# Threshold attention followed by a maxout FFN on one core: both r of a quad share one pass over the ninth keys

## The chip, the cores and the metric

The kernel runs on one core of one Trainium2 chip. Times are device microseconds of one execution of the whole program, and the figure of a version is the median of its runs.

## The reference

```python
# attn: q, k, v are (8, 8, 576, 64) f32, tau = 0.02
scores = scale * np.matmul(q, k.transpose(0, 1, 3, 2))          # scale = 1/8
thresh = np.max(scores, axis=-1, keepdims=True) - tau
scores = np.where(scores >= thresh, scores, -1000000000.0)
scores = scores - np.max(scores, axis=-1, keepdims=True)
attn = np.exp(scores)
attn = attn / (np.sum(attn, axis=-1, keepdims=True) + 1e-09)
o = np.matmul(attn, v)
# ffn: x is o as (4608, 512); w1, w2, w3 are (512, 768), w_out is (768, 512)
h = np.maximum(np.maximum(x @ w1, x @ w2), x @ w3)
out = h @ w_out
```

Each of 64 heads (8 batches of 8) takes a 576 by 576 softmax in which only scores within tau of the row's maximum count. The FFN works on the 576 tokens of each batch, 512 wide.

## The kernel before

**Tiling.** A batch is split into two quads of four heads. In a quad, heads are numbered 2r + i, with r = 0, 1 and i = 0, 1. The 576 tokens of a batch lie nine to a partition (64 partitions of nine), so that the first eight make four chunks of 128 and the ninth tokens make a chunk of 64. For a quad there are nine steps of scores: four chunks of 128 queries for i = 0, one step that takes the ninth queries of both i (64 rows each), and four chunks for i = 1. Each step has two halves, r = 0 and 1.

**A half of scores (S).** `scores` multiplies queries with all 576 keys in f32. The keys lie in two row halves of PE (partitions 0 to 63 and 64 to 127), 320 and 256 of them, and the two halves of the array run side by side into two PSUM banks. The trace prints the shape of the array as 64*128. The step of the ninth queries is split by columns as well, 64*64. The result `sc` is 128 by 576.

**Softmax.** `maximum` (m, on DVE) writes z = -sc with the row's minimum beside it. Then one of two ways, set for each half by a digit in `MASKED`. Unmasked: `threshold` (s, DVE, a small instruction), `exponents` as a Prelu with a very small slope (e, ACT) and `numerators` as an Exp with a running sum (n, ACT). Masked: `exponents` as an Exp (e, ACT) and `numerators` as a compare and multiply with a sum (k, DVE). So an unmasked half costs two passes over 128x576 on ACT and one on DVE, a masked one costs one on ACT and two on DVE. Digits 2 and 3 are the same two ways with the e step reading `sc` from PSUM (2 has no threshold step). Then `reciprocals` (r, DVE), and `normalized` (p, POOL) writes `P` in bf16. When both r are there, a DMA on SP turns `P` (t) into `ptq`, a tile of 128 by 9 by 1152: nine chunks of 128 keys, 576 queries for each i. Chunks 0 to 3 hold the keys of r = 0, chunks 5 to 8 those of r = 1, and chunk 4 holds the ninth keys of both, r = 0 in partitions 0 to 63 and r = 1 in 64 to 127.

**The product (O).** `product(L, r, ...)`, line 415, makes the output of one r. It goes over five chunks: m = 0 to 3 with weights `vb` (v of the eight tokens, cast on POOL) and m = 4 with `vrb`, the v of the ninth tokens. i = 0 goes to PSUM partitions 0 to 63 and i = 1 to 64 to 127, so the array is 128*64, and the two i run side by side. Since chunk 4 holds the keys of both r, `vrb` has zeros in the rows of the other r (three buffers `vr0` to `vr2`, lines 244 and 661 to 666, zeroed once by DVE; `cast_v` fills the rows). Each pass runs over 576 query columns as 512 and 64, since a PSUM bank holds 512. The result `o` is copied to `xt` by DVE for r = 0 (w) and by ACT for r = 1 (x).

**FFN.** `hid` makes `ph` for each of six blocks of the hidden width and three weights. Both 64-row halves of the contraction run side by side (64*128), in two steps F and B with the halves exchanged. ACT copies the first (h), DVE takes the maximum (v). `outp` makes `po`, which ACT copies to `ob` (u) for the store (o). The last batch (7) is split in two parts of 256 and 320 tokens (`SPLIT`), whose FFN has the shapes 128*128.

**PSUM.** Four tags `s0` to `s3` of 1024 f32 columns, two banks each; this document calls such a tag a bank pair. Every S, T (transposes of q and k, `tp`), O and F step takes the pair that the digit behind its letter names, and waits until its last user has been read.

**The order.** Nothing schedules at run time. `ORDER` is one string of letters; `issue` (line 719) takes them one after the other, and `_Ordered` (line 84) keeps each engine to that order. `products` (line 692) hands out the O steps, two per quad (r = 0, then r = 1), and in the string other letters can stand between the two. The other letters are a, c (copies of `tp`), q (swaps on POOL), y (casts of v), l, g (loads), z (weight casts), i, d (stores) and N, j (the ninth tokens' outputs). All instructions show line 93 in the profile, since `_Ordered` issues them; they are told apart by their tiles.

Of the kernel before, what the change touches and what calls it, by code (L numbers as in the profile page):

```python
# [12 lines left out]
BF16 = mybir.dt.bfloat16  # L13
# [8 lines left out]
FLAT = 2.0 ** -100  # L22

MASKED = """
232222322322222222021032222202332122123122200200111000000000100000000011
000010111020011000101000000001100001001000010011111100000000100100000000
110010030111000100010000000001010100001110001011010100110000000000000000
100101101011000000120000001010000000110011100000001110001000010011111021
"""


# [6 lines left out]
SPLIT = {7: ((0, 1), (2, 3, 4))}  # L38

ORDER = """  # L40
llllllglllT0laclT1laclzllqqS0qqS1meS2mS3lmlT0enlkS1ylmlT2eamelrnpS3leqlmnyS1qcapS0emtnrcS3pmnT2qmepgrelS1qya
gS0pmelT2mqnS3tcpemqS2nlkT1eytaS0rmnT1kpermS3yS2enczrmS1qT0enmepnqtS3nprmaymgpeS0lptS2mppT0mtpS1enencnqsS3re
rmtpS0mS1penmS3lqnsS2mtperpekzllmT0tmpenkT1pgS3eearnS0petmnqrS2meqlnpS3lmnplsS2cetpremS1pS0nmplermtzeS3mnS2p
mtnpmS3rkpS1leektS0emnrpmemptS1eekS2pO3mktS0rennmpermT2pnS1wptemS3prkyO0tmeakS2pgS1enxlnrmS0lpesS2mezT3mS1np
mgntspcS2eqrseT3mtpeS0srmapS1mnT2ptS3mnqO0ceqmeO1prswnptnkS3pxS0meF1meS2zBresmT0qghF3klpF2nkBtaS1sveS0pemF3B
nyrrsmyBepT1svS0hpcT2nS3zmaS1erpgsF2mntpsBmnS3yvF1etssT0myeBprS2cnpS3mnS0ympelF2epF3lmBnzslssvS0htBrqmeS2vpn
S1gF0sepmF3teqBmF2erssvpBtnBkphF0eS1vtS3znmF2nrBmqteS1rpvBnS3pmlnF0pmgeS1qsBsrhmS3pevS2npS1mF0npsO3ermpesmO2
zewepgsskBxtT3nF1vS2nklBarS0mlphS3mtepF2sS1rmnyBmetF3pvT0eBpcnS2tzT1nvS0asmzS3temS2qeS1meF0trkpmS3lenpBmnlys
reklpF1umerpskS3upBeoketmS0uS2umpS3tesmS1qeT0myO2nqlrsnlprcO3etqsmepwS0xptS1mnF3psnmS2BlerskpS1thF0meF3pmeBF
2ktnBveBsrS1nvpS0hmyF3emF2npBrssT0eprtvBaF1kS3nqvBeF0myhyS2kyleF3mBelBvnpS2snsS0vptemS1pnF3rmpT2tnBmpeF0scS1  # L50
htBrnmpF3erT2rpvlBasS1pstvnS2pmeF0pS3emtBqnmT2S1hcqS3empF2eS0rsqmtS1epsmBeF3pmnF0stsvBeBknF2klhF1BvelS0nrvpB
emT3pS2arvS0ptnS3mpnO1smtesrkpeF2swnlrpmeT0S1qtescS3epBmnpmnT0trskS3paS1umS0ulqmeS3lmyS1nopS2smelS0rmeS3psmn
O1ypersmqO2etkpemO0lewqxlknpS3tS1keF2momS3lexF0ktT1enkBercpnsBpumN1ertkphkF3jS0rursS1empBnmF2ptS0vpS1smeF3yt
BsnsmBpnvS0pT1hmF2atT3srepS0cF1eprBsmeqF3vnByBynvplS2nsS0plmhS1mteS2mF0nF3mteS1rrspBnmS2pelvBlepF1smT0leqBvl
aS2rkhF3oqnsS0mtS1epmBeqsF2ssmtS0epvBeyF1mnF3vpBesrS0ktphBermS1npT2svO0nytmpncT3eS1wF2nrmS0aBrsmnqF3vnT1pS0c
eBptsF2mhpS1eS3pmteS0qmBeO1spmnkteF3rvnpT0BsskapS2xvS0erS1qmtnS3pmnF2mqlespmeS1rtkBepresmT3puS1cuS0ptmnS3pS2
meyS1lrekpF0tnsmempO3lekteskO2nrsmpeBkpxrnwS1uptS3muS2pnmF0yoeS1mF3lesymBtnS2srkpS1hmBeF0spveF2ertBmpT3nrsvS
1paBlmpnS0tS3qhmF1epsmS2leBymF3tevF0nBknlS1rsvpS2esmqnBF3srmhpS1epS0tmeF2pssBrempBtesvS0ynF1mT3lnpBvF0lhsrcS
2tnT1mBnF3valS2nrBsqmeF0pvS1epS2meBptsmS3eqF1hmT2peBcS3tnskT2O0arkplnmO2lerpvewptS3xkpS1nF2meF0sstreBsmpS3nv
pBnmS1tS2hmT3eF0rmpnF1cBpnBrevptT3S2apvS0qmtS3S1enmqF2esrsqmiepmleS0soykeS1plBnmemtS3ukS0uT1snrlO2cpekynO1me  # L60
ymeF3pwxskteS0keS1BrrnkopmF2pmS0BqeuurtsmF1phS3srnpS2meT0ptBmeS3ykpaN2esvempF0tS1jkpF3ermBeS2ptvnS1pmBnS0rls
hsmpS2elF3mqntS1mpF0nsrBskpeF2lsmBetBpveF1yhvS3lnkS2lesF0mytnBmBerqsS3veF2lpvnF1pBsmT0htBceF3rT2vnpBsaS0pvnF
1qmtS2nBsrnmT0pS3hrcpF2esS1mpteS0rmpS3emBpntF1svqnS0ssBmpeoT2vO3lamtneF1wS0nrlBpmeS3qsrS2hsmS0pnmF1eptS3smeB
pmF2ntS0veS3rsmnpS1BnpO0veytrempS2empS3xsmS1tekF0nsknlT2rmpBelmlpnscS3quS1umyS2eorT0kpeO3tmeyO1ewlepsmF3etka
rknS2qklT0nBmxespcS2eryF0mpF1uskpuBtnS2BhmqF3nsvS0peS2srmtpF1eBmpeF0srvnBptS2hyS3pmeF1lmeBlBevtF3nkT2S0arrvp
BnS2mphS1smpF0ntS3smnpBmeF1lsT2esvlF3nrBrcptBnvpS2eS0qmlhS1tsnprsmT3F2epmS0aptBemF3yevS1oS0nqmBnpsrS2mnF1ptv
S0epmBeS3mthS2skeF0F1snmlBeklO3ersvpnrmByepF0swT2eqtBvnqF3ssrcS1hpiBmpT0S2vaptS1snmS0pnT3mqF2tecT1BarmS3pnS1
vqeS0mF2pesrmnptmS3npT1seS0qctBeymqermpS1eS3mpuF0nmtuskS1eS2klnS3smBesrsepO1upmemO2txrkpukeO3wnkpS0xS2emF3et
rmS1pnBssspmF2hS0rtepS3mnBpmF1etS0veF3mnN2rnpBpjF0evtF2esBkBkhF1nsvS3eBmBevO3hrkS2pwnS1mnF3prmS2eptsF0mnBpsS
1sevyS2terBmpeF3svS1iyepBmoS0yhmtF2ekF3nBsmS1ersBvpnF0pmeF2BvteS1hBmF3rsS0vpeF1rknpBBmnO2vhptO0xrpnS3pwS2trm  # L70
npS0mnF3pmteF1pBeBvtS0rS2vpS3empF1ktkF0kBereskpemBkperumO2uptO3xpN1wtenkO2jrF3pxF1hpF2nvF3tvF1rhF2pvF3pvF1hF
2tvF3vF1hF2voF3vF1ohF2vF3vF1hF2vO3vO1wF2xuuF1oF0hiF3vF1vF0hF3vF1vF0hF3vF1vF0hF3vF1vF0hF3vF1vF0huF3vF1ovF3uoF
0uoN1fjdi
"""


# [28 lines left out]
def kernel(  # L105
# [34 lines left out]
    one = ctx.enter_context(tc.tile_pool(name="one", bufs=1))  # L140
# [100 lines left out]
                               in_=v[b].rearrange("h (p c) d -> p c h d", c=9)[:, 8])  # L241
                yield

    vrs = [one.tile([128, 4, D], BF16, name=f"vr{x}") for x in range(3)]

    def cast_v(L):
        L["vb"] = vp.tile([128, 4, 4, D], BF16, name="vb")
        pool.tensor_copy(out=L["vb"], in_=L["vm"])
        yield
        L["vrb"] = vrs[(2 * L["b"] + L["qd"]) % 3]  # L250
        for r in range(2):
            rows = slice(64 * r, 64 * r + 64)
            pool.tensor_copy(out=L["vrb"][rows, 2 * r:2 * r + 2], in_=Ls[2 * L["b"]]["vr"][rows, 4 * L["qd"] + 2 * r:4 * L["qd"] + 2 * r + 2])
            yield

    def half(n, i):
# [155 lines left out]
            L["pt"] = pt_pool.tile([128, 9, W], BF16, name="ptq")  # L412
        sync.dma_start_transpose(out=L["pt"][:, :, c["idx"] * 128:(c["idx"] + 1) * 128], in_=c["P"])

    def product(L, r, target, part=None):

        pt, vb, vrb = L["pt"], L["vb"], L["vrb"]
        st = {}

        lo, hi = span(part)  # L420
        n = min(hi, 512) - lo
        base = 448 if ninth_first(L["b"]) else 0
        if ninth_first(L["b"]):
# [218 lines left out]
    Ls, xts, stores, stores9, ends, ninths = {}, {}, [], [], [], []  # L642
# [147 lines left out]
    x = 0  # L790
# [39 lines left out]
```

## Time and profile before

| | |
|---|---|
| runs | 446.49, 447.15, 447.59 us; median 447.15 |
| the profiled execution | 446.69 us, of which its span is 444.8 |
| granted TensorE clock, mean | 0.988 |
| busy: PE, PEld, DVE, ACT, POOL | 422.4, 320.2, 392.8, 403.0, 311.9 us |
| products: `o` from `vb`, `o` from `vr` | 544 and 136 matmuls |

Busy time is the union of the instructions of an engine, and the ends of matmuls are modelled: a matmul's row is longer than its share of the array, and successive rows overlap. Starts are the better guide to what a matmul costs. PEld is the weight load, which overlaps PE. A form such as 128*64 is the tile shape of the array, rows by columns; 128x512 is partitions by elements of the moving operand.

### The profile page before, as it was taken

Reading aid. Unit: us, or ns where it says so; the run is one execution under the profiler, and the core shown is the slowest. Engines: PE = TensorE matmul, PEld = TensorE weight load, DVE = VectorE, ACT = ScalarE, POOL = GpSimd, SP = SyncE. Lnnn points to the kernel's source line nnn. Section 1 sums busy time; section 2 is a strip of 40 time slices with the busy share of each in tenths; the row PEclk is TensorE's granted clock in tenths of the full one; section 3 lists DMA queues with packets and bytes.
Section 4 is the critical chain, followed back from the end, with each engine's and each line's share of the span. In section 5 each row is a group of like instructions: output and inputs, shape, how many; then the busy total and the mean of one; then the engine's idle time right before and its main releaser. Section 6 shows DMA issues by size and latency. Waiting matters only on the chain.

```text
span 444.8 us, 14254 instructions
## 1 busy us (share of the span) xinstructions
PE 422.4 (95%) x5188; PEld 320.2 (72%) x5190; DVE 392.8 (88%) x1228; ACT 403.0 (91%) x836; POOL 311.9 (70%) x420
## 2 busy tenths in 40 slices
PE   7767789999999999999999999999999999999996
PEld 6334347787788767787788777788688886787873
DVE  3887999999999999999999999998999998899642
ACT  3999999999999999999999999899999999987632
POOL 2799989997878687696785877676676685457400
PEclk8998999999999999999999999999999999999999
DMA  7999999999999999699899999989999977487633
GB/s 188 275 293 199 291 169 269 235 243 262 229 180 194 212 222 292 125 256 167 143 234 189 230 198 203 209 168 210 208 206 194 244 151 105 83 179 136 145 116 108
DMA packets 213959, 88.50 MB, mean 199 GB/s; under 512 B 189184, under 2 KB 202240, under 8 KB 213888
## 3 DMA queue, kind: packets, MB, share of 16 engines
q1 hardware_dynamic: 213360, 86.96, 95.9%
q8 instruction: 41, 0.67, 0.6%
q10 hardware_dynamic: 528, 0.62, 0.5%
q14 instruction: 30, 0.25, 0.2%
HBM read 35.65 MB, written 9.44 MB: 101 GB/s over the span
## 4 chain that ended last, share of the span: by engine, by line
PE 86%; ACT 5%; DVE 4%; issue 2%; DMA 1%; SPq 0%; DVEq 0%; ACTq 0%
PE ph L93 32%; PE sc L93 32%; PE po L93 10%; PE o L93 9%; ACT z L93 5%; PE tp L93 3%; DVE z L93 3%; DMA qm<-in_q_dram 1%; ACT qt L93 1%; SPq L93 0%; DVE xt L93 0%; DVE hm L93 0%; DVE stage L93 0%; DVE rs L93 0%; ACT ob L93 0%
## 5 line engine op out<-in xcount | busy, mean ns | idle before, releaser
L93 POOL TENSOR_SCALAR P<-z,rs 128x576 bf16<-128x576 f32 x250 | 200.6, 814 | 63.3 <-DVE rs L93 28.1
L93 DVE TENSOR_SCALAR_CACHE_REDUCE z<-sc 128x576 f32<-128x576 f32 x250 | 183.7, 750 | 14.8 <-PE sc L93 10.1
L93 PE MATMUL sc<-kt,qs 64*128 64x256 f32 (+2 forms) x640 | 182.6, 423 | 5.7 <-DVE z L93 2.3
L93 PE MATMUL sc<-kt,qt 64*128 64x320 f32 (+2 forms) x640 | 182.4, 433 | 5.2 <-ACT z L93 3.3
L93 PE MATMUL ph<-xt,w 64*128 64x288 bf16 (+2 forms) x2160 | 170.8, 283 | 0.1
L93 PEld LDWEIGHTS <-w 64*128 64x128 bf16 (+1 forms) x2160 | 130.1, 94 | 28.6 <-issue 4.3
L93 ACT ACTIVATE z<-z 128x576 f32<-128x576 f32 x174 | 117.6, 679 | 0.1
L93 PEld LDWEIGHTS sc<-kt,qs 64*128 64x128 f32 (+1 forms) x640 | 92.4, 180 | 25.7 <-DVE z L93 5.7
L93 ACT ACTIVATE z<-z,th 128x576 f32<-128x576 f32 x143 | 106.2, 769 | 5.0 <-DVE th L93 4.2
L93 PEld LDWEIGHTS sc<-kt,qt 64*128 64x128 f32 (+1 forms) x640 | 91.9, 179 | 19.7 <-ACT z L93 5.9
L93 DVE SCALAR_TENSOR_TENSOR z<-z 128x576 f32<-128x576 f32 x76 | 62.2, 830 | 0.5 <-ACT z L93 0.5
L93 PE MATMUL po<-wo,hT 64*128 64x512 bf16 (+3 forms) x454 | 53.5, 354 | 0.3
L93 POOL COPY qs<-qt 64x640 f32<-64x640 f32 (+3 forms) x66 | 43.0, 652 | 10.8 <-ACT qt L93 7.2
L93 ACT ACTIVATE z<-z,nm 128x576 f32<-128x576 f32 x68 | 50.6, 767 | 0.0
L93 DVE TENSOR_TENSOR hm<-ph,hm 128x576 bf16<-128x576 f32 (+2 forms) x54 | 37.0, 686 | 9.2 <-PE ph L93 8.9
L93 ACT ACTIVATE hm<-ph 128x576 bf16<-128x576 f32 (+2 forms) x54 | 31.8, 589 | 13.4 <-PE ph L93 12.8
L93 POOL TENSOR_SCALAR P<-stage,rs 128x576 bf16<-128x576 f32 x38 | 30.4, 804 | 19.3 <-ACT z L93 5.4
L93 PEld LDWEIGHTS <-hT 64*128 64x128 bf16 (+2 forms) x456 | 30.0, 95 | 16.5 <-issue 2.3
L93 DVE TENSOR_TENSOR hT<-ph,hm 128x576 bf16<-128x576 f32 (+2 forms) x54 | 37.0, 686 | 4.0 <-PE ph L93 2.3
L93 PE MATMUL o<-ptq,vb 128*64 128x64 bf16 (+2 forms) x544 | 39.0, 281 | 0.0
L93 ACT ACTIVATION_READ_ACCUMULATOR z<-z 128x1 f32 x174 | 34.3, 197 | 0.0
L93 PEld LDWEIGHTS <-vb 128*64 128x64 bf16 x544 | 23.3, 111 | 12.8 <-issue 4.9
(45 smaller groups left out, 431.6 us busy)
## 6 DMA issues: line engine op xcount, KB each, us to landing
vm<-in_v_dram SPq DMA_DIRECT2D x32, 256.0 KB, 4.8
qm<-in_q_dram SPq DMA_DIRECT2D x15, 512.0 KB, 5.0
km<-in_k_dram SPq DMA_DIRECT2D x15, 512.0 KB, 5.3
out_dram<-ob SPq DMA_DIRECT2D x14, 512.0 KB, 4.0
stage<-in_moe_w_dram SPq DMA_DIRECT2D x9, 512.0 KB, 5.2
ptq<-P SPq DMA_TRANSPOSE x144, 4.0
vr<-in_v_dram SPq DMA_DIRECT2D x16, 128.0 KB, 3.4
stage<-in_moe_w_out_dram SPq DMA_DIRECT2D x3, 512.0 KB, 4.9
```

Source lines behind the costliest of these rows:

```text
L93: ins = fn(*a, **kw)
```

## The change

`product` makes four passes for each r. The ninth keys of both r are done in one pass after the four of r = 1: r = 0 in rows 0 to 63 of the array and r = 1 in rows 64 to 127, each i in its own 64 columns, thus four matmuls in 64*64 quadrants for each run of columns. Rows 0 to 63 write the bank pair that r = 0's step took, rows 64 to 127 that of r = 1, so r = 0's result is complete only after r = 1's step. `vrb` needs only two heads' width and no zeros: each half of its partitions holds the two heads of its r. `start` is set for the first matmul in each bank alone. `MASKED` has other digits and `ORDER` is another string with the same letters but for four (86 k and 202 n become 90 and 198, and 169 s become 168).

```diff
@@ MASKED, ORDER: new strings (not shown) @@
-    vrs = [one.tile([128, 4, D], BF16, name=f"vr{x}") for x in range(3)]
+    vrs = [one.tile([128, 2, D], BF16, name=f"vr{x}") for x in range(3)]
...
-            pool.tensor_copy(out=L["vrb"][rows, 2 * r:2 * r + 2], in_=Ls[2 * L["b"]]["vr"][rows, 4 * L["qd"] + 2 * r:4 * L["qd"] + 2 * r + 2])
+            pool.tensor_copy(out=L["vrb"][rows], in_=Ls[2 * L["b"]]["vr"][rows, 4 * L["qd"] + 2 * r:4 * L["qd"] + 2 * r + 2])
...
-    def product(L, r, target, part=None):
+    def product(L, r, target, part=None, other=None):
...
-        order = [(m, run) for m in range(5) for run in runs] if part is None else \
-            [(m, run) for run in runs for m in range(5)]
+        order = [(m, run) for m in range(4) for run in runs] if part is None else \
+            [(m, run) for run in runs for m in range(4)]
...
             for m, (*q0, p0, n) in order:
+                opens = m == 0 and (p0 == runs[0][2] or p0 // 512 != runs[0][2] // 512)
                 for i in range(2):
-                    w = vb[:, 2 * r + i, (1, 3, 0, 2)[m], :] if m < 4 else vrb[:, 2 * r + i, :]
-                    tensor.matmul(ps[64 * i:64 * i + 64, p0:p0 + n], w,
-                                  pt[:, 4 if m == 4 else m + 5 * r, q0[i]:q0[i] + n],
-                                  start=(m == 0), stop=(m == 4))
+                    tensor.matmul(ps[64 * i:64 * i + 64, p0:p0 + n], vb[:, 2 * r + i, (1, 3, 0, 2)[m], :],
+                                  pt[:, m + 5 * r, q0[i]:q0[i] + n], start=opens, stop=False)
+            if other is None:
+                return
+            for *q0, p0, n in runs:
+                shuts = p0 == runs[-1][2] or p0 // 512 != runs[-1][2] // 512
+                for x, two in ((0, other.st["ps"]), (1, ps)):
+                    rows = slice(64 * x, 64 * x + 64)
+                    for i in range(2):
+                        tensor.matmul(two[64 * i:64 * i + 64, p0:p0 + n], vrb[rows, i, :],
+                                      pt[rows, 4, q0[i]:q0[i] + n], start=False, stop=shuts)
...
+        p.st = st
...
-    plain = vrs[2].rearrange("p h d -> p (h d)")[:, 0:128]
+    plain = vrs[2].rearrange("p i d -> p (i d)")
     vector.memset(vrs[2], 0.0)
-    for t in vrs[0:2]:
-        for x in range(2):
-            vector.memset(t[64 - 64 * x:128 - 64 * x, 2 * x:2 * x + 2, :], 0.0)
...
                 for g in (2 * b, 2 * b + 1):
-                    for r in range(2):
-                        yield product(Ls[g], r, x_of, part)
+                    p = product(Ls[g], 0, x_of, part)
+                    yield p
+                    yield product(Ls[g], 1, x_of, part, p)
```

More of the change, by code (lines that the diff above doesn't have):

```diff
@@ L24 @@
 MASKED = """
[L25 to L28, printed above, removed]
+032222120132222220001212222202110312323122222200113000000010000000100001
+000010011010011000011000000010100001011000110001011110000000100010000010
+110000001110000101010000000101001000001001011001031020011000100000000010
+001100111100001000000002001010000000011110101001100010110000001101011122
 """
@@ L40 @@
 ORDER = """
[L41 to L70, printed above, removed]
@@ L71 @@
-npS0mnF3pmteF1pBeBvtS0rS2vpS3empF1ktkF0kBereskpemBkperumO2uptO3xpN1wtenkO2jrF3pxF1hpF2nvF3tvF1rhF2pvF3pvF1hF
-2tvF3vF1hF2voF3vF1ohF2vF3vF1hF2vO3vO1wF2xuuF1oF0hiF3vF1vF0hF3vF1vF0hF3vF1vF0hF3vF1vF0hF3vF1vF0huF3vF1ovF3uoF
-0uoN1fjdi
+lllllllgllT0laclT1qqS0lacllzlqqS1msS2emS0lmelT3nlkT1lyrmlS2eaacqlcqS3mlqS1yenmnpS0mpemS1ytS2enrqmpT3nmS1pler
+sS2pleklpaS0gmnT3teqrmeqclpemS3ngkpS1temT2myT0teacS2qrenkynS0mqeS3rmpnS1ymprenT3ptmS2npsS1ersmzetT0mS2epT1al
+pmnS3lyscnleS0qrmtepS3epmgnS2pktzeamS1leknS0qnrmepnS3ptmprmS2preemtpT1mS3ptenncS0npsrS1mepmtS3eqmS0ezS2nkT1p
@@ new lines @@
+nrmnpstmeqemS0prklptS3emeankpS1gemlerS2kptrmS0penmeS3ptmnpreS1mpelS2mqtS0kpO3emS1rktpmO2enkqgenemnlS0rlnwplx
+rprS3mteS2pmnT0pS1mntT3psmS2apersS1cepS3meO0zmekpO1gmtkzS3T2enxswntS1ceF0psrF2meqlBmnqgF3rhsBktyeT1svByaF0pv
+nT2pS1rncS3pterBmpS2hsmF1petT0sS3mpaBepsmF0eT2zvBncF3pgnS1vlS2ynrmBtnS0pmhS1sysmeS2zremF0pgS3esmtBpesmF2pnS1
+vBqesmF0nyF3klnBsstrS1vepBmhpF2nrlvS0pnS1lmpBelrmS3zetS0vF1nqmF2nptBmeS3qssBhkqgF0evS1eBrpssmeS2pmnO3pveS1rn
+mpF0nmS2zeBmS1pgnssrkO2tyhesmeS0wtpF1esS3pmxBtyremS2pnF0vpT3estmT1zBacS2ezsvtS3emT1qnS0tF2nrmpnmpS3nlS0qmnlB
@@ new lines @@
+rseklpatkF3epemS1urqmS0ueBpokntyS1mupS2usrmlS0peT3lsmeO1qtcnpO2mestkS3xwS0erlsmF1pnS2sspmeBF3rtkhpF0emBnkF1p
+lBnvBerrtS2vphS3mpS0nmF1pteS2mpeBmT0nlF3rsskpeF2tBvaBespvF1onS0ktF3hrmBpeF2rvqeT0BsnycBnsvS0peS1rmqthS3mpeS0
+smF2eypT1mBaptS3snvS1ynmT0qF2nlmpF3elBrscpS1elvyS0nlmBteF2pmF1hsskBnBtsveS3rF0revpF2ekqBnS1mBhmpF3espvS0tnS1
+pmeT2BmytayS0rvnpS1S2semqT3nmO0percptS1mpF3emtenskT2eS1kBarknpmS2urpsS1sumepS3tmepS2mnS1mlS3erslssO2pmelmqek
+S1ptxS3nsmS2ermtO1pewpeO3mylnkleS0ylF2xwtqermpeT3S1cnpBmnqtrkepS3S1umoN0eyskpuemS3F2nrstsmpF1jBkpeF0klhBekF3
@@ new lines @@
+BnsvBrtS2vphS1mepF3mnlS0BsnlrmpF1elsT2vpBatsrF3pvnT2S0prnclByemS1leS2tmpS0hmpF1reslsS2mnpBtmnpS0evS3yqF2smln
+T1qBtmeF0vaT3eBciF2ekS3lhS1rstsmpnBmqS0eS3vpeF1srnmtF2pBnmpBevS3qthsF0mnT1BrkpeF3vaT2BscpeF1rtnS0svpBempS3hr
+S2lymnS0plmS1etqF3mnS2pmeF0trBsempBnsvpT2oO1evteO3knsrkapS0nwF2xmpeskytS1nS0rrmeS3pssemS1pBemptnmT0puS3cuS1y
+tmeqS0S2mnqS3semlyF1nrmpeskO0pesmO2eqktnnS3wBxrkpermS0upS2srsumS3eptmF1epS0mS2epmtBnpsF3mhS0srleBpmT1lnpF2vt
+eS0kS3amBntF1veF0ssBmnBlrekF3pohF2kleBvBespS1vhS0trmepS2rnmpS1nS3smptF0essmqF2nBmpleS1svlS3nBlrmpnF0lrsF1npm
@@ new lines @@
+tBepvT3BhsycF2elrS0vyteS3pmeT1pBmaoF0qevT1tS3npcBsnkF1lS2hrmtpBemT0qnS3vF2qnmO1pesketO3kaesrrpBwxS0ynsvpS1eS
+3mptF2nmqS0nrmBpS1mhqS3temF2pT0snmS1perBscptF3evT0peBsmyS2ntvS1nmF3elskelrS2meplBmnpkatS1uS0umT2eO3slcesrkO1
+permepkS2nF0qtxsemS1pewBympenrkS3ptuS1muS2nmpS0eN3sqmtermpeF2kF0ynBkjS1hT3pmBaS2sstrvepS3reF1mpS0nompF2lnmBp
+F3etvqS0nsBmnS1trsBhkpF0esvF2eBmyeBrkF1phS3vnS2mpntS0mepF3mBelT2srsevF0ptBnrcpF1ekBpoBvhlS2ntpvF3nT0mBaS1rrt
+svpeF2mT0qnS3sclpBesS1lmphS0tmeqF2mnS3pBsnrlssmpF0etS1vqeBmS2evT3F1amS0nsS3qmeS2prBsmnF0ptmhS3qerBssmS2pevS1
@@ new lines @@
+eptS3mnF0ympS2nBtmnO1rvepsnO3kpemeS0rwtpS2xmpnS1smF0lerktepT2knS3meBlcpnmeS1tS2usrmpF3espmeT1sutkO2erkpaO0kl
+nleS1wyxBpsemtnkT0F1urcpS2ulrS0epmoS3nqBstmeF2ysmT0hBqaF3veyS1psS0nmpBerF2kptnF1vBemBphS3srnrtvpS2eF0mpS1nml
+pF3nBssmpeBsrvF1peT2hBycplF0nvS3leBsmelF1vlS2nBtemS0nrsS2pmhS3tqmeF1smpnS2lBqemS3tervS0pF2nsmpT1tnBmyF3avS0e
+tS1keF2rmnpBsBmqhF0rnspssS3veBptmF2epvT1S3nqctBemS0hT1srkF3poaS2meBmqnF0sS1vpnS2rmntpT3BsempO1ercptnvT2qS3as
+S0pnmS2qtemS3yermF0pemqeT2pS3nBtmnrcepS3uF2pmutekS3rS0skpeBimlkpO3eusmukeS0twxS2nmO1ekO0rssrpempS3xwptS2emF1
@@ L74 @@
+pnmS0onF3rkpBtmS2hBpmnN1sevteskS2jS3meF0rF1smepBrnkpBS3hS2meptS1mpF3mF2tBvBennrsrvpeS0F1eyvF3yemBS2pshS0mynt
+ByspemF1S2epsvBemtF0F3skeBvF2hBsskF0rvBpBkpF3hS1veF0mtnBrBnpvS1nopS2veF3trmS0pnBmpeO1mhO2tsknS3rwS0pmeF1pnmF
+3ektBBxrvpeS0sS2pevS1nmtF3rkpemF0rpmBkptS2piBmekN1enkO3euuotreuurpO2jO0pwxO1pntnpF2wF3htF0vF2rvpF3hF0xpvF2vF
+3thF0vF2vF3hoF0vF2ivF3hF0vF2vF3hF0vO2vO3F0xwF2F3hF1vF2vF3hF1vF2vF3hF1vF2vF3hF1vF2vF3hF1vF2vF3huF1vF2ovF1uoF3
+uoN2fjdi
 """
```

## The prediction

> **What bounds the kernel now.** The page comes first: busy time, the slices, and the chain that ended last.
>
> ```profile
> span 444.8 us, 14254 instructions
> ...
> PE 422.4 (95%) x5188; PEld 320.2 (72%) x5190; DVE 392.8 (88%) x1228; ACT 403.0 (91%) x836; POOL 311.9 (70%) x420
> ...
> PE   7767789999999999999999999999999999999996
> ...
> ACT  3999999999999999999999999899999999987632
> ...
> PE 86%; ACT 5%; DVE 4%; issue 2%; DMA 1%; SPq 0%; DVEq 0%; ACTq 0%
> ```
>
> Three engines are near full, so the average doesn't settle which one counts. The busy times by stretch do (columns: PE, PEld, DVE, ACT, POOL, granted clock, DMA).
>
> ```profile
> core 0: us, PE busy (x) PEld busy (x) DVE busy (x) ACT busy (x) POOL busy (x), PEclk, DMA share, GB/s
> ...
> 20.00:40.00 20.00, 13.68 (x112) 8.59 (x112) 17.18 (x51) 18.89 (x42) 18.76 (x27) 0.91 1.18 245
> 40.00:60.00 20.00, 15.37 (x122) 7.95 (x120) 17.78 (x56) 20.00 (x44) 17.20 (x22) 0.91 1.16 256
> ...
> 120.00:140.00 20.00, 20.00 (x292) 17.44 (x290) 18.95 (x62) 19.95 (x43) 15.36 (x21) 1.00 1.21 216
> ...
> 300.00:320.00 20.00, 20.00 (x254) 15.61 (x251) 18.62 (x62) 19.64 (x42) 12.80 (x20) 1.00 1.10 204
> ...
> 400.00:420.00 20.00, 20.00 (x253) 16.05 (x248) 15.52 (x47) 14.28 (x33) 13.52 (x17) 1.00 0.64 120
> ```
>
> There are three stages. Up to about 73 us there is only attention of the first batch or two, ACT is full (20.00 of 20 at 40 to 60 us) and PE idles for a quarter of the time. From 73 to about 390 us PE and ACT are both full and DVE nearly. In the last 50 us PE alone is. The chain of waits dates the border: the last product pair of batch 0, and the first FFN (ph) behind it.
>
> ```profile
> 69.46 2.59 PE o L93 x40
> 72.05 1.17 PE sc L93 x8
> 73.22 0.50 PE ph L93 x8
> ```
>
> What PE waits for between 80 and 400 us is little:
>
> ```profile
> PEld L93 <- issue: 8.4, 30, 0.4
> ...
> PEld sc L93 <- issue: 3.3, 11, 0.4
> PEld sc L93 <- DVE z L93: 3.0, 11, 0.5
> ...
> PEld sc L93 <- DVE hm L93: 2.2, 5, 1.3
> ...
> PEld sc L93 <- ACT z L93: 0.4, 1, 0.4
> ```
>
> Only 5.6 us of the lower three rows are waits for another engine in 320 us; the idle put down to "issue" belongs to PE itself. So PE time taken out after 73 us can come off the end nearly whole, as long as ACT and DVE, as full as PE in the middle, don't take its place.
>
> **The removed pass.** A product of one r streams five passes over the 576 queries: four over its own keys and one over the ninth keys, in which half of the rows meet zeros. The rows of those ninth passes, and of the timeline where two products follow each other:
>
> ```profile
> L93 PE MATMUL o<-ptq,vr 128*64 128x512 bf16 x56 | 11.5, 382 | 0.0
> ...
> L93 PE MATMUL o<-ptq,vr 128*64 128x64 bf16 x64 | 7.0, 193 | 0.0
> L93 PEld LDWEIGHTS <-vr 128*64 128x64 bf16 x136 | 6.2, 111 | 2.2
> ```
>
> ```profile
> 99.89 1.19 PE L93 MATMUL o<-ptq,vb 128*64 128x512 bf16 x15
> 100.91 0.38 PE L93 MATMUL o<-ptq,vr 128*64 128x512 bf16 x1
> ...
> 102.14 0.38 PE L93 MATMUL o<-ptq,vr 128*64 128x512 bf16 x1
> ...
> 102.53 0.66 PE L93 MATMUL ph<-xt,w 64*128 64x288 bf16 x8
> ```
>
> The durations (382 ns) overlap and can't be added. The starts can be read: the ninth pass of r=1 begins 102.14 - 100.91 = 1.23 us after that of r=0, five passes later, so a pass is worth 0.247 us. There are 14 full pairs (seven batches, two quads) and four in the split batch 7, two of 256 and two of 320 columns, together two more full passes. Removed: 16 x 0.247 = **3.95 us**. The shared pass keeps as many matmuls as the two had; it gains only if its four 64*64 quadrants run at once. The trace has such a shape, the scores of the ninth tokens:
>
> ```profile
> 84.80 0.43 PE L93 MATMUL sc<-kt,qs 64*64 64x256 f32 x2
> 84.81 0.49 PE L93 MATMUL sc<-kt,qt 64*64 64x320 f32 x2
> ...
> 85.40 0.38 PE L93 MATMUL sc<-kt,qs 64*64 64x256 f32 x2
> 85.55 0.43 PE L93 MATMUL sc<-kt,qt 64*64 64x320 f32 x2
> 85.62 0.38 PE L93 MATMUL sc<-kt,qs 64*64 64x256 f32 x2
> 85.93 0.30 PE L93 MATMUL ph<-xt,w 64*128 64x288 bf16 x2
> ```
>
> All four start within about 0.02 us, so four at once it is, and I take one pass for the shared one. (The Trainium skill, "TensorE: Matmul & The Clock Gate", Part 3, measured 3.07 times for four row tiles and not 4. As an estimate from that page the shared pass would take 4/3.07 = 1.30 passes, 1.2 us less gain over the kernel; no run here shows bf16 quadrants.)
>
> **The changes of shape.** PE pays when it goes from one tile shape to another. In the last fence two matmuls of 256 columns in one shape start 85.62 - 85.40 = 0.22 apart, but the ph behind the second starts 0.31 after it: 0.09 us for the change. From above: the ten passes and one exit between 99.89 and 102.53 take 2.64 us, ten passes are 2.47, so at most 0.17. I take 0.12, nearer to the direct reading. Following the written orders step by step with the shape of each, the old one has 76 changes; the new one has 71 between steps (five fewer, since more pairs stand back to back) and 18 more inside the products, where 128*64 goes to 64*64: 89. That adds 13 x 0.12 = **1.6 us** (1.2 to 2.2). Nothing hides it in a stage where PE is full.
>
> **Moved between ACT and DVE.** MASKED goes from 86 masked halves of scores to 90. A masked half does one pass fewer on ACT and one more on DVE; th also falls from 169 to 168. The pitch of both, from 56 us on:
>
> ```profile
> 55.68 0.71 ACT L93 ACTIVATE z<-z 128x576 f32<-128x576 f32 x1
> ...
> 56.35 0.70 ACT L93 ACTIVATE z<-z 128x576 f32<-128x576 f32 x1
> ```
>
> ```profile
> 55.80 0.75 DVE L93 TENSOR_SCALAR_CACHE_REDUCE z<-sc 128x576 f32<-128x576 f32 x1
> ...
> 56.48 0.75 DVE L93 SCALAR_TENSOR_TENSOR z<-z 128x576 f32<-128x576 f32 x1
> ```
>
> A pass is 0.67 us on ACT and 0.68 on DVE. ACT loses 4 x 0.67 = 2.7 us, DVE gains 2.7. ACT is full in the middle, and falls by about what PE falls, so it doesn't hold PE up; DVE had 1.0 to 1.4 us free in each 20 and covers 2.7 over 317 us. Without that cover the 2.7 would come back whole.
>
> **The head.** It is set by ACT, so O passes saved there (two pairs) bring little. Before the first FFN step the old order has 54 scores and 87 exponent passes on ACT (50 first and 37 second ones), the new one 55 scores and 87 (52 and 35); copies on ACT are equal, DVE has three masked passes more (2.0 us, of which 20 - 17.18 and 20 - 17.78 lie free). So ACT reaches the first FFN at the same time, with one score more behind it (about 0.5 us of PE), which pays for the two pairs' saving that the head swallows (0.5 minus their two shape changes). Net zero, by -0.5 to +0.5.
>
> **Small edits.** Four memsets on DVE go (0.4 us in all) and one gets narrower; they lie in the first 2 us, beside the wait for the first q:
>
> ```profile
> 2.43 4.67 DMA qm<-in_q_dram
> ```
>
> ```profile
> L93 DVE MEMSET vr<- 64x64 uint32 x4 | 0.4, 112 | 0.2
> ```
>
> The casts of the ninth v keep count and size. The cast of r=0's result on DVE now waits for the shared pass behind r=1, and so does the release of its PSUM bank. Where the pair is back to back, the cast comes about 1.2 us later; PE has the other two of the four bank pairs, two steps of about half a us, against a cast of 0.67 us on DVE and the copy of r=1 on ACT beside it. That covers it barely; the price without it is the second rival.
>
> The re-written order moves loads, transposes (SP) and POOL's steps too. The number of each is the same; their places shift by some steps. Bound: nothing to the few tenths of a wait in the fence of waits.
>
> **Sum.** -3.95 + 1.6 + 0 = -2.35 us. The profiled execution took 446.69 us (span 444.8), so 444.3 for its like; the median of the three runs, 447.15, lies 0.46 above, hence **444.8 us**.
>
> **Rivals.** (1) The three engines are so evenly full that PE's saving is eaten by waits for z and hm: the middle then lasts as long as ACT and DVE need. For it: 19.95 and 18.95 of 20. Against it: ACT sheds 2.7 us too. Half to all of 2.35 is lost: 446.0 to 447.2. Chance 0.17.
>
> (2) Slower: a pair that isn't back to back now holds r=0's bank until r=1's pass has ended. In the new order four pairs stand apart (batch 0, 1, 2 and 6, first quad), with 1, 5, 11 and 14 steps between, 27 of which open a bank; they have three bank pairs in place of four, and PE waits sooner for DVE or ACT to empty one. The old order had eight pairs apart, but freed the bank early. Price per wait, from the whole run:
>
> ```profile
> PEld sc L93 <- DVE z L93: 8.9, 18, 1.8
> ```
>
> 8.9/18 = 0.49 us. Nine such waits (every third step) cost 4.4 us and end at 449.2. It turns to slower from 8 on: (2.35 + 1.34)/0.49, where 1.34 us is 0.3%, about what a measurement can tell from no change here. For it: PE steps already reuse banks within one or two steps. Against it: only 18 waits of this kind occur now in 288 scores. Chance 0.18, with what else a re-written order can lose.
>
> (3) The weight loads of the shared pass aren't hidden. Two rounds of loads (for 512 and for 64 columns) of 111 ns in each full pair are 0.22 us, over 18 pairs 3.7 us: 448.5. Against it: the old pass has four loads of 111 ns in 0.247 us, so they overlap there. (That a load overlaps a running matmul only when their row groups differ is what the Trainium skill says, "TensorE: Matmul & The Clock Gate", Part 3, "What overlaps and what doesn't"; the trace of the 128*64 passes disagrees with it as worded, since all their loads and matmuls share the same rows.) Chance 0.05. That the quadrants go two by two, so that nothing is saved and the changes of shape are paid, would give about the same, 448.7; the score rows all but exclude it.
>
> **How the numbers follow.** The forecast has 0.60. Its own ends: changes at 0.09 and at 0.17 give -2.75 and -1.75, the head adds 0.5 either way, and with no price for changes at all it is -3.95; the runs of one kernel spread by half a us. So 442.7 at the low end. Above, the range takes in rivals 1 and 3 and rival 2 up to nine waits: 449.3. Faster by over 0.3% (under 445.8): 0.56, the forecast less 0.04 for its weak end. Same: 0.25 (rival 1, that 0.04, most of rival 3). Slower: 0.19.
>
> **What would show it.** Right: 128*64 matmuls from vr are gone, and 64*64 ones from vr stand in their place, four starting within some 0.02 us; from the first ninth matmul of the shared pass to the next step about 0.35 us; the first ph near 73 us; PE full from there to the end, which comes 2.4 us earlier; ACT 2.7 less busy and DVE 2.7 more. Wrong: the first ph over a us later (the head, by ACT or POOL), new rows "sc <- DVE xt" or "sc <- ACT xt" of some us (rival 2), waits for z up by some us from 80 to 400 us (rival 1), or a shared pass of 0.5 us (rival 3).

## The result and the profile after

| | median, us | lowest to highest, us | runs |
|---|---|---|---|
| before | 447.97 | 446.49 to 450.43 | 8 |
| after | 451.27 | 450.48 to 452.39 | 8 |

The ratio is 1.0086 (95% interval 1.0067 to 1.0105): slower by 3.9 us, where 2.35 us of gain were forecast, and above the top of the range (449.3). The ratio is estimated over all fast runs and isn't the quotient of the two medians, which lie 3.3 us apart; us that are given for a ratio here are that ratio times the median before. The profiled execution of the changed kernel took 451.33 us. Its page, first the span, the busy times, and the chain that ended last:

```profile
span 449.5 us, 14304 instructions
...
PE 423.9 (94%) x5190; PEld 317.9 (71%) x5190; DVE 396.8 (88%) x1231; ACT 402.3 (89%) x828; POOL 317.6 (71%) x420
...
PE 77%; POOL 7%; ACT 4%; DVE 3%; issue 3%; DMA 2%; SPq 1%; POOLq 0%; DVEq 0%; ACTq 0%
```

POOL wasn't among the engines of the chain before; now it has 7% of it. DVE is 4.0 us busier, ACT 0.7 less, POOL 5.7 more. The stretches that the prediction read (PE, PEld, DVE, ACT, POOL, granted clock, DMA):

```profile
20.00:40.00 20.00, 13.50 (x116) 8.14 (x116) 15.96 (x51) 18.72 (x40) 19.23 (x25) 0.91 1.10 233
40.00:60.00 20.00, 14.20 (x98) 7.54 (x90) 18.30 (x59) 19.84 (x43) 19.23 (x23) 0.91 1.08 250
120.00:140.00 20.00, 20.00 (x277) 15.65 (x275) 19.50 (x62) 19.26 (x39) 14.86 (x20) 1.00 1.15 215
300.00:320.00 20.00, 20.00 (x253) 15.22 (x251) 19.25 (x64) 19.79 (x42) 15.22 (x20) 1.00 1.05 195
400.00:420.00 20.00, 19.39 (x255) 14.69 (x250) 15.54 (x49) 17.69 (x40) 12.61 (x16) 1.00 0.96 181
```

In the head (20 to 60 us) POOL is busy 19.23 of 20, up from 18.76 and 17.20; in the middle DVE is up to 19.5 and 19.25. The first FFN matmul in the timelines of before and after:

```profile
73.06 0.67 PE L93 MATMUL ph<-xt,w 64*128 64x288 bf16 x8
```

```profile
75.57 2.73 PE L93 MATMUL ph<-xt,w 64*128 64x288 bf16 x40
```

So 2.5 us are lost by then, and from there to the end of the span it takes 449.5 - 75.57 = 373.9 us instead of 444.8 - 73.06 = 371.7. From here on the time up to the first FFN matmul is called **the head** of a run, and the time from it to the end of the span **the rest**. The shared pass, in the timeline of PE and in the groups by form (mean ns of one behind the comma):

```profile
105.91 1.18 PE L93 MATMUL o<-ptq,vb 128*64 128x512 bf16 x16
107.02 0.44 PE L93 MATMUL o<-ptq,vr 64*64 64x512 bf16 x8
107.39 0.53 PE L93 MATMUL sc<-kt,qt 64*128 64x320 f32 x1
```

```profile
L93 PE MATMUL o<-ptq,vr 64*64 64x512 bf16 x56 | 5.7, 400 | 0.0
...
L93 PE MATMUL o<-ptq,vr 64*64 64x64 bf16 x64 | 3.2, 189 | 0.0
```

It does what was forecast: eight matmuls of the ninth keys, four of 512 columns at 400 ns each, all end within 0.44 us, and the next step starts 0.37 us after the first of them. The same step of the old product on the same order (the first experiment below) has one ninth pass of its own there, and the same scores behind it:

```profile
105.17 1.18 PE L93 MATMUL o<-ptq,vb 128*64 128x512 bf16 x16
106.18 0.41 PE L93 MATMUL o<-ptq,vr 128*64 128x512 bf16 x4
106.53 0.53 PE L93 MATMUL sc<-kt,qt 64*128 64x320 f32 x1
```

From its first ninth matmul to the next step it is 0.35 us, so the shared pass takes about 0.02 us longer than one old pass, if the change out of either costs the same. The change into its shape costs 0.10: 107.02 - 105.91 = 1.11 us against 106.18 - 105.17 = 1.01 for the four passes ahead of it. The union of the 512-column rows fell from 11.5 to 5.7 us, that of the 64-column rows from 7.0 to 3.2. So the loss lies elsewhere. What PE waits for between 80 and 400 us has moved from hm to z and to small steps of DVE:

```profile
PEld L93 <- issue: 10.9, 38, 0.5
...
PEld sc L93 <- DVE z L93: 5.0, 14, 1.0
...
PEld sc L93 <- issue: 3.7, 14, 0.4
...
PEld sc L93 <- DVE stage L93: 1.9, 6, 0.5
...
PEld sc L93 <- DVE rs L93: 0.8, 2, 0.4
PEld sc L93 <- DVE kt L93: 0.8, 3, 0.3
```

The two issue rows are 14.6 us, 2.9 more than before; the same order with the old product, which lacks the added changes of shape, has 11.5. The rows for DVE z, stage, rs and kt are 8.5 us; before, z and stage had 3.4 and the other two none. All rows of this view in which PE waits for DVE come to 9.0 us before, 12.4 for the old product on the new order, and 12.5 after.

### The profile page after: what moved, and what is told of

Its sections match the earlier page's. It is cut to its first block, busy times and chain, and to the rows that moved or that the text cites. A ratio compares the mean times of both kernels' runs of the same rounds, so it can differ in the third digit from the quotient of the medians.

```text
span 449.5 us, 14304 instructions
## 1 busy us (share of the span) xinstructions
PE 423.9 (94%) x5190; PEld 317.9 (71%) x5190; DVE 396.8 (88%) x1231; ACT 402.3 (89%) x828; POOL 317.6 (71%) x420
## 4 chain that ended last, share of the span: by engine, by line
PE 77%; POOL 7%; ACT 4%; DVE 3%; issue 3%; DMA 2%; SPq 1%; POOLq 0%; DVEq 0%; ACTq 0%
PE ph L93 30%; PE sc L93 27%; PE po L93 9%; PE o L93 7%; POOL P L93 4%; ACT z L93 4%; PE tp L93 3%; DVE z L93 3%; POOL qs L93 2%; DMA vm<-in_v_dram 2%; SPq L93 1%; DMA out_dram<-ob 1%; POOL vb L93 1%; POOL w L93 0%; POOL vr L93 0%
## 5 line engine op out<-in xcount | busy, mean ns | idle before, releaser
L93 DVE TENSOR_SCALAR_CACHE_REDUCE z<-sc 128x576 f32<-128x576 f32 x250 | 183.4, 751 | 17.5 <-POOL P L93 7.9
L93 PE MATMUL sc<-kt,qt 64*128 64x320 f32 (+2 forms) x640 | 184.5, 432 | 2.3 <-DVE z L93 1.6
L93 PE MATMUL ph<-xt,w 64*128 64x288 bf16 (+2 forms) x2160 | 168.8, 283 | 0.3 <-DVE z L93 0.2
L93 PEld LDWEIGHTS <-w 64*128 64x128 bf16 (+1 forms) x2160 | 127.0, 94 | 29.8 <-issue 4.7
L93 ACT ACTIVATE z<-z 128x576 f32<-128x576 f32 x173 | 116.4, 675 | 0.1
L93 DVE SCALAR_TENSOR_TENSOR z<-z 128x576 f32<-128x576 f32 x77 | 65.0, 853 | 0.5 <-ACT z L93 0.4
L93 POOL COPY qs<-qt 64x640 f32<-64x640 f32 (+3 forms) x66 | 46.7, 708 | 10.7 <-ACT qt L93 6.8
L93 ACT ACTIVATE z<-z,nm 128x576 f32<-128x576 f32 x70 | 52.7, 766 | 0.1
L93 PEld LDWEIGHTS <-hT 64*128 64x128 bf16 (+2 forms) x456 | 32.8, 95 | 15.4 <-issue 2.2
L93 POOL TENSOR_SCALAR P<-stage,rs 128x576 bf16<-128x576 f32 x38 | 31.5, 835 | 13.6 <-DVE rs L93 10.1
L93 PE MATMUL o<-ptq,vb 128*64 128x512 bf16 (+2 forms) x544 | 36.4, 281 | 0.6 <-ACT ob L93 0.6
```

Of the source, the lines that this page charges most:

```text
L93: ins = fn(*a, **kw)
```

## The experiments

Each ratio is to the kernel before, measured beside it. Heads and rests come from one profile each. Three kernels with the head of after have their first ph at 74.9 to 75.6 us, and four with the head of before at 72.9 to 73.2, so a few tenths in a head say nothing.

**The old product with the new order.** The code of before, with ORDER and MASKED of after:

```diff
 # the kernel before
-MASKED, ORDER of before
+MASKED, ORDER of after
```

> The old product (two ninth passes with zeros) on the new ORDER and MASKED; the result is that of the reference. Theory A (the new order loses the time, the shared pass itself is worth about what was forecast): slower than the changed kernel by some 2.4 us, about 453.7 us, ratio to before 1.013. Theory B (the shared pass loses the time, by its changes of shape and the late release of r=0's bank): about as before, 447 to 449 us, ratio 1.000 to 1.003.

Measured: 1.0139 (1.0122 to 1.0156), 452.60 us against 446.61.

```profile
span 450.0 us, 14307 instructions
...
74.59 2.73 PE L93 MATMUL ph<-xt,w 64*128 64x288 bf16 x40
```

The order and its digits alone cost 1.39%, 6.2 us (5.4 to 7.0): 1.5 us in the head and 3.7 in the rest (375.4). On this same order the shared pass takes 1.39 - 0.86 = 0.53% back, 2.4 us (1.2 to 3.5 from both intervals), against 2.35 forecast. The timelines show where: from the first matmul of a pair's products to the step behind them, summed over both products, the twelve full pairs of the rest are 0.12 to 0.22 us shorter, 1.7 us together, and the rests differ by 375.4 - 373.9 = 1.5. The head doesn't share in it; in these two profiles it is even 1.0 us later with the shared pass. The gain is there, and the order costs more than it.

**The shared pass on the old order.** ORDER and MASKED of before, the shared pass only in the ten pairs that stand back to back there:

```diff
+    TOGETHER = (1, 2, 3, 5, 7, 8, 9, 11, 13, 17)
...
-        order = [(m, run) for m in range(5) ...
+        M = 4 if both else 5        # both: this pair is in TOGETHER
+        order = [(m, run) for m in range(M) ...
```

> The old ORDER and MASKED; the shared pass only in the ten pairs whose two products stand back to back there (nine of 576 columns, one of 320: 9.6 passes), the other eight as before, so no step moves. Theory A: 9.6 x 0.247 = 2.4 us saved, ten changes of shape added at 0.12 us, so 1.2 us faster, ratio 0.997. Theory B: ten of eighteen parts of a loss of 3.3 us, 1.8 us slower, ratio 1.004.

Measured: 1.0075 (1.006 to 1.009), 449.92 us. At seven of the ten pairs the step behind the products comes 0.12 to 0.14 us sooner after their first matmul than before, the pass less the shape change; at two (near 101 and 427 us) it is 0.01 to 0.03. Then, a few steps on, more is lost. The tenth pair, at 324 us in the timeline, of all engines:

```profile
324.04 0.44 PE L93 MATMUL o<-ptq,vr 64*64 64x512 bf16 x8
...
324.52 0.76 DVE L93 CAST xt<-o 128x576 bf16<-128x576 f32 x1 [1.64 <-PE o L93]
...
325.19 0.14 DVE L93 TENSOR_SCALAR th<-nm 128x1 f32<-128x1 f32 x1
...
325.33 1.47 PE L93 MATMUL po<-wo,hT 64*128 64x512 bf16 x12 [0.85 <-DVE th L93]
```

The copy of r=0's result (w) is next in DVE's order, and DVE stands still for 1.64 us until the shared pass has ended; what is queued behind it is late, and PE then waits 0.85 us for DVE. Such waits of w, in the whole run of before, after, the old product on the new order, and this kernel:

```profile
DVE xt L93 <- PE o L93: 2.3, 5, 1.2
```

```profile
DVE xt L93 <- PE o L93: 5.6, 8, 1.9
```

```profile
DVE xt L93 <- PE o L93: 1.2, 3, 0.8
```

```profile
DVE xt L93 <- PE o L93: 7.6, 11, 1.6
```

**The late result taken away, on both orders.** The kernel of the last experiment, with w moved behind one or two more large steps of DVE in seven pairs (the text below says eight; ORDER moves it in seven), and each step given the bank pair that the written order releases first; and the same order with the old product, as a control:

```diff
-ORDER: ... w (right behind the second O) ...
+ORDER: ... w behind the next one or two of m, k, v, c; digits behind S, T, O, F chosen anew
```

> As the run with the shared pass in ten pairs of the old order, but r=0's cast (w) stands behind the next one or two large DVE steps in eight of these pairs, and from the first of them on each step takes the bank pair whose last user is read out first by the written order. Theory A (the shared pass is worth 0.12 us a pair on PE, and the earlier run lost only because DVE stood at a cast that now comes 1.1 us later, 0.2 to 1.64 us each time): 1 to 1.2 us faster than the kernel before, ratio 0.997. Rival (a result 1.1 us later costs as much wherever the cast stands): 1.004 to 1.007, as the earlier run.

> The order and banks of the run before with the old product: the control. Theory A: the moved casts and banks cost 0 to 0.5 us by themselves, ratio 1.000 to 1.001, and the shared pass gains 1.2 us against it. Rival: this one is 0.997 or less too, so that the gain is that of the banks.

Measured: 1.0006 (0.9991 to 1.0022) and, the control, 1.0014 (0.9995 to 1.0033). The waits of w are gone but for 2.6 us in four, about what the kernel before has, and 0.69% comes back: on the old order the late result, with the bank pairs that it makes scarce, accounts for the loss within these intervals. Which of the two edits gave how much wasn't tried. The two kernels don't differ beyond their intervals, so the 1.2 us that ten shared passes should gain isn't resolved here. The same two edits on the changed kernel, w moved in the four pairs where it waited 0.28 to 0.54 us in the middle:

> The changed kernel, with the copy w of r=0's result moved behind one more large step of DVE in the four pairs of the middle stage where it waited (0.53, 0.28, 0.54 and 0.44 us), and each step's bank pair chosen anew: the one that the written order releases first. Theory L (the late result of r=0 and banks released late are a large part of the loss): it gains as much as the same two edits gained on the old order with the shared pass in ten pairs, 0.5 to 0.7%, so 1.002 to 1.004. Theory P (the places of the other steps cost, which these edits leave): 1.006 to 1.009.

Measured: 1.0094 (1.0074 to 1.0113), 451.69 us. The waits of w fell from 5.6 to 3.2 us (between 80 and 400 us from 2.0 to 0.2) and nothing came back; a new wait of PE for w's copy, 1.0 us, came with it. So in the middle of the changed kernel the late result isn't what costs by itself. The waits outside the middle were left as they were, and the old product on this order wasn't tried.

**Old head with new rest, and the reverse.** The old product, with the one order up to the first FFN step and the other behind it:

```diff
-ORDER = one string
+ORDER = letters of one order up to the first F, then the other's that are still to come; MASKED alike
```

> The old product; ORDER and MASKED up to the first FFN step are those of the kernel before, and behind it the new ones, less what was issued already. The new order with the old product was 1.0139. Theory D (by its trace, 1.5 us are lost up to the first FFN step and 3.6 behind it): 1.008 to 1.010. Rival (the head is the cause, and what follows is its echo): 1.000 to 1.003.

> The reverse: the new order up to the first FFN step, the old one behind it, the old product. Theory D: 1.003 to 1.006. Rival of the run before: 1.010 or more. If neither half alone costs much, the cost lies in their meeting: both near 1.002.

Measured: 1.0157 (1.0131 to 1.0183) and 1.0143 (1.0117 to 1.0169). As whole kernels they decide nothing: at the seam the order fits neither part, the first ph came at 78.14 and 77.57 us, and from 20 to 60 us the granted clock was 0.74 and 0.83 in the first one where the kernel before has 0.91. Their rests do say something: 375.0 us with the new order and 372.4 with the old one, where the whole kernels had 375.4 and 371.7. So the new rest costs 3.7 us behind its own head and 2.6 in these two.

**DVE against POOL.** The masked numerators (k) read z twice and so take two operands from SBUF. Here k reads z once (it writes the outcome of the compare, the multiply by z is left out), first on the new order and then on the old one:

```diff
-            vector.scalar_tensor_tensor(out=z, in0=z, scalar=thr, in1=z,
-                                        op0=OP.is_ge, op1=OP.mult, accum_out=acc)
+            vector.tensor_scalar(out=z, in0=z, scalar1=thr, scalar2=None,
+                                 op0=OP.is_ge, op1=OP.add, accum_out=acc)
```

> The changed kernel with the masked numerators (k on DVE) as a compare with a sum, which reads z once in place of twice; the values are other ones, the number and size of instructions are the same. Theory C (the new head is late because DVE's two-input k and POOL's reads of SBUF hold each other up, and POOL ends last there): P beside a k falls from 1.19 to 0.75 us, the first FFN step comes at 73 us or earlier in place of 75.6, and the kernel ends 2.5 us or more earlier than the changed one, 448.8 or less. Rival (the order's places alone make the head late): no change in the first FFN step's time beyond 0.5 us, 450.5 to 451.5.

> The kernel before with the same one-input k. Theory C: it gains less than the changed kernel does by the same edit, since POOL isn't last in its head: 0 to 1 us, 446.5 to 447.5. Rival: both gain the same, whatever that is, and the distance of about 3.5 us between the two kernels stays.

Measured: 0.9994 (0.9974 to 1.0014) on the new order, 0.92% less than the changed kernel, and 0.9931 (0.9912 to 0.9951) on the old one. The heads: 71.03 us (4.5 less) and 71.10 (2.0 less). The groups by form up to 75 us, in the changed kernel and then in the same with one operand:

```profile
L93 POOL TENSOR_SCALAR P<-z,rs 128x576 bf16<-128x576 f32 x46 | 37.8, 836 | 1.2 <-DVE rs L93 0.3
L93 DVE SCALAR_TENSOR_TENSOR z<-z 128x576 f32<-128x576 f32 x15 | 14.6, 973 | 0.5 <-ACT z L93 0.4
L93 POOL COPY qs<-qt 64x640 f32<-64x640 f32 x6 | 6.3, 1050 | 0.4
```

```profile
L93 POOL TENSOR_SCALAR P<-z,rs 128x576 bf16<-128x576 f32 x48 | 35.1, 745 | 4.7 <-DVE rs L93 1.3 <-DMA ptq<-P 1.2 <-PE sc L93 1.1
...
L93 DVE TENSOR_SCALAR_CACHE_REDUCE z<-z 128x576 f32<-128x576 f32 x16 | 11.9, 745 | 0.7 <-ACT z L93 0.6
...
L93 POOL COPY qs<-qt 64x640 f32<-64x640 f32 x6 | 4.3, 714 | 0.4
```

P falls from 836 to 745 ns in the mean, qs from 1050 to 714, k from 973 to 745. Alone a k is no shorter with one operand: the shortest of each kernel take 0.73 us. So k and POOL's steps hold each other up. The kernel before has some of it too, in the same stretch:

```profile
L93 POOL TENSOR_SCALAR P<-z,rs 128x576 bf16<-128x576 f32 x46 | 37.2, 823 | 3.7 <-DVE rs L93 2.6
L93 DVE SCALAR_TENSOR_TENSOR z<-z 128x576 f32<-128x576 f32 x12 | 11.5, 962 | 0.5 <-ACT z L93 0.5
L93 POOL COPY qs<-qt 64x640 f32<-64x640 f32 x6 | 4.7, 780 | 0.4
```

What the new order adds is three more k and longer qs; P is hardly longer. The holding up can be read step by step in the timeline of the changed kernel:

```profile
36.30 0.72 POOL L93 COPY qs<-qt 64x640 f32<-64x640 f32 x1
...
39.82 1.03 POOL L93 CAST w<-stage 128x1024 bf16<-128x1024 f32 x1
39.95 1.51 DVE L93 SCALAR_TENSOR_TENSOR z<-z 128x576 f32<-128x576 f32 x1
...
40.91 1.13 POOL L93 COPY qs<-qt 64x640 f32<-64x640 f32 x1
```

This k starts at 39.95 beside a cast on POOL that ends at 40.85. If it stood until then and ran the 0.75 us that its row has alone, it would end at 41.60; it ends at 41.46. The qs behind it starts at 40.91; if that stood until k's end and then ran the 0.72 us that it takes alone, it would end at 42.18; it ends at 42.04. That is what the Trainium skill says ("SBUF — State Buffer", section "SBUF: two separate sides"): a DVE step with two SBUF inputs and a GpSimd step that reads SBUF take one port pair in turn, for the whole step. These rows agree with it to 0.15 us. Up to 75 us the new order has 15 such k, the old one 12. And DVE then waits for POOL, since a buffer of z is free only after P; up to 75 us, before and after:

```profile
DVE z L93 <- POOL P L93: 1.2, 2, 1.0
```

```profile
DVE z L93 <- POOL P L93: 4.9, 6, 2.0
```

The difference of the two heads is this contention: with one-operand k both are 71.0 to 71.1 us. POOL isn't the limit of the whole new head; in the chain of waits its steps have most of the time from 15 to 43 us, and ACT's z most of that from 44 to 60. The rest isn't explained by it: 372.3 us on the new order and 369.6 on the old, still 2.7 apart.

**Fewer masks in the new head.** The changed kernel with three masked halves of the head (halves 9, 30 and 39) turned back, nothing moved:

```diff
-MASKED: 1 at three halves; k at their places
+MASKED: 0 at three halves; n in place of k, and s ahead of their e
```

> The changed kernel, with three masked halves of the head turned back to unmasked at their places. Theory C (in the head, DVE steps with two inputs from SBUF and POOL's steps hold each other up, and POOL sets the head's end): 0.3 to 0.45 us per step on POOL come back, the first ph 0.9 to 1.4 us earlier than its 75.6 us, ratio 1.005 to 1.007. Theory A (ACT sets the head's end, as the prediction had it): ACT gets three passes of 0.67 us more, the first ph 1 to 2 us later, ratio 1.010 to 1.013.

Measured: 1.0095 (1.0076 to 1.0114), the first ph at 74.75 us. ACT has 2.5 us more up to 80 us (71.42 for 68.94) and the head isn't later, so ACT's total doesn't set it. POOL has 2.6 us less (63.54 for 66.12) and the head is 0.8 us earlier, hardly outside the spread of such heads, while the ratio didn't fall; neither theory's numbers came. (From 40 to 60 us the granted clock was 0.83 in this profile and 0.91 in that of after, which can hide a small gain.)

**The share of DVE in the rest.** The prediction let DVE cover four more masked halves. On the old order, four halves spread over the middle turned to masked (81, 134, 189, 243), nothing moved:

```diff
-MASKED: 0 at four halves; n at their places, s ahead of their e
+MASKED: 1 at four halves; k in place of n, no s
```

> The kernel before, with four halves of scores in the middle stage (spread evenly over it) turned from unmasked to masked, at the places where they stand; nothing else moves. Theory M (the new digits of MASKED are what costs in the middle: four halves more there sit on DVE, each 0.68 us of DVE more and 0.67 us of ACT less): the middle gets about 2.7 to 3 us longer, ratio 1.006 to 1.007. Theory P (the places of the steps cost, not the share of DVE): within 0.3% of the kernel before, 0.999 to 1.002.

Measured: 1.0057 (1.003 to 1.0085), 449.59 us.

```profile
span 447.7 us, 14245 instructions
...
PE 425.1 (95%) x5190; PEld 321.1 (72%) x5190; DVE 396.6 (89%) x1232; ACT 401.2 (90%) x828; POOL 313.5 (70%) x420
...
73.20 0.67 PE L109 MATMUL ph<-xt,w 64*128 64x288 bf16 x8
```

The rest is 447.7 - 73.20 = 374.5 us, 2.8 more than before, for 4 x 0.68 = 2.7 us of DVE. No cover shows. The mirror of it, four masked halves of the middle of the changed kernel turned back:

> The changed kernel, with four masked halves of the middle stage turned back to unmasked, so that the middle has as many as in the kernel before; nothing else moves. Theory M (the digits cost in the middle): 2.7 to 3 us come back, ratio to the kernel before 1.002 to 1.003, against the 1.0086 of the changed kernel. Theory P (the places cost): 1.007 to 1.010.

Measured: 1.0129 (1.0105 to 1.0153), 453.06 us, slower than the changed kernel by 0.43%; the rest is 375.5 us. So taking DVE's share back doesn't give the time back, and both theories missed. Two more runs on the old order then change digits without DVE's total, and take from DVE (the edits are as above: 80, 135, 188 and 242 back to unmasked, with and without the four turned to masked):

> The kernel before, with the same four halves turned to masked as in the run with four more, and for each of them a neighbouring masked half turned back (80, 135, 188 and 242 for 81, 134, 189 and 243), so that DVE and ACT keep their totals everywhere within one step of scores. Theory D (DVE's total is what cost 0.57% there, since it has no room in the middle): 0.999 to 1.002. Theory F (the order is fitted to its digits, and each digit that differs costs its pass wherever it goes): 1.005 to 1.011.

> The kernel before, with those four neighbouring halves (80, 135, 188 and 242) turned from masked to unmasked, nothing else: DVE 2.7 us less, ACT 2.7 us more in the middle. Theory D (DVE is what binds): 0.996 to 1.001. Theory F, or ACT as full as DVE: 1.004 to 1.007.

Measured: 1.0031 (1.0015 to 1.0047) and 1.0017 (1.0001 to 1.0033); rests 373.0 and 372.4. Neither theory's numbers came. The exchange, which leaves both totals, costs 1.4 us (0.7 to 2.1); four passes from DVE to ACT cost 0.8 (0.0 to 1.5); four from ACT to DVE 2.5 (1.3 to 3.8). So the old order is fitted to its digits: each of these changes in the middle made it slower, the one that adds to neither engine too. DVE seems to have less room than ACT beyond that, but these intervals don't tell how much less.

## Why the prediction was wrong, point by point

The term that failed is the new order with its digits: the prediction put it at nothing to a few tenths, and the old product on the new order measured 6.2 us. The term for the shared pass came out as forecast.

**What bounds the kernel.** On the new order PE time saved after 73 us came off the end: 1.7 us at the pairs, 1.5 in the rest. On the old order it didn't: the same pass in ten pairs ended 0.75% later, since DVE stood at w. So PE's time counts only as long as the other engines' orders don't wait for the changed step. The fence of waits from 80 to 400 us, in which the prediction saw 5.6 us for other engines, left rows out: PE's waits for DVE alone were 9.0. That ACT sets the head isn't borne out: up to 85 us the chain of waits of the kernel before has 27.5% on PE's scores and 25.2% on ACT's z, and the one of after 26.3% on POOL's P and qs and 17.5% on ACT's z.

**The removed pass and the shape changes.** Right: 0.247 us of pass less 0.12 of change is the 0.12 to 0.14 us seen at most full pairs, and the quadrants run four at once. The 3.07 of the Trainium skill ("TensorE: Matmul & The Clock Gate", Part 3) would, as an estimate, make the shared pass 0.07 us longer than one old pass and leave about 1.2 us of gain. The pair at 106 us shows 0.02 us longer, which is nearer to the full four; the whole gain, 2.4 (1.2 to 3.5), excludes neither. The count of shapes was a little short: by the starts in the timelines PE changes its shape 76 times before, 74 with the old product on the new order and 91 after, 15 more and not 13, or about 0.2 us.

**The head, "net zero, by -0.5 to +0.5".** Wrong: +1.5 us with the old product, +2.5 in the profile of after. The step that failed is "So ACT reaches the first FFN at the same time". It counted passes by their own durations and left out that a k holds up POOL and POOL holds up a k. With three k more and qs at 1050 ns for 780, the passes that were to lie free on DVE also cost POOL, which was busy 19.23 of 20 us there, and DVE's waits for POOL's P rose from 1.2 to 4.9 us.

**The cover of DVE, "1.0 to 1.4 us free in each 20 and covers 2.7".** Wrong on the old order, where it could be tried: four more masked halves cost 2.5 us (1.3 to 3.8), nearly what the text gave for no cover (2.7). But exchanging four for four costs 1.4 without more work for DVE, so part of the 2.5 is the misfit of digits and order. Free time in a stretch of 20 us was taken for room. The experiments fit the reading that it lies in gaps between steps that wait for each other, but that is argued, not shown.

**The re-written order, "nothing to the few tenths of a wait".** Wrong by the most: 6.2 us with its digits, of which the head has 1.5 and the rest 3.7 by the profiles. The rest's share goes with many short waits of PE for DVE, which are 12.4 us for the old product on the new order and 9.0 before. What makes these waits stays open, and so does how much of it is digits and how much places of steps: four more digits on DVE cost 2.5 us on the old order, but giving four back on the new one made it slower.

**The rivals.** Rival 2 named the right direction (slower, at 449.2, 2 us short; "with what else a re-written order can lose") and one right mechanism in the wrong place. A late r=0 does cost, on DVE and in back-to-back pairs, 0.7% on the old order; in the changed kernel moving its copy in the middle brought nothing, and PE's waits for DVE's xt there are 1.9 us in the whole run. Rival 1 saw the middle full, but had waits only eat the saving. Rival 3 fell: the loads of the shared pass aren't seen in its 0.37 us. Of what the prediction said would show it wrong, two signs came: the first ph over a us later, and waits for z up between 80 and 400 us (PE's scores for DVE's z from 3.0 to 5.0).

**The sum in its terms.** Order and digits cost 6.2 us where nothing was forecast, the shared pass with its shape changes brings 2.4 where 2.35 was. That these two come so close is in part luck, since the interval is 1.2 to 3.5. The second is the difference of two measured ratios, so that these two close on the measured 3.9 by their making; the profiles of one execution each (5.2 us of span for the first, 0.5 for the second) lie below both, within what runs of one kernel differ.

No version with the same result beats the kernel before; the shared pass with late casts equals it. That one-operand k gains 0.7% on the old order shows what is lost to the port, but it computes something else.

## What to carry to other kernels

Price a hand-written order as a term of its own: when an edit comes with a new order, run the old code on the new order, for the edit and its order can have opposite signs. The free time of an engine that is 93 to 95% busy beside two full ones isn't room for more work until the places of that time are shown. When the result of a step comes later, look first at the engine whose fixed order has the reader of it next, and not only at the buffer that it holds.

## What the runs showed of the hardware

A DVE step with two SBUF operands and a POOL step stop each other for whole steps: qs 0.72 us alone and 1.13 beside a k, k 0.75 alone and 1.51 beside a cast of POOL. All k with one operand instead made this kernel 0.7% faster on the old order and 0.9% on the new one. And bf16 quadrants of 64*64 run four at once: eight matmuls, four of them of 400 ns, within 0.44 us, and the change from 128*64 into them took 0.10 us.
